# Asking for a block's rows at the head of the step, copying row numbers a block ahead, and placing filter pieces in the first half of the second product

## The chip, the cores and the metric

The kernel runs on one core of a Trainium2 chip. A core has a matrix engine (TensorE, PE in the profile; PEld are its weight loads), three engines for elementwise work (VectorE or DVE, ScalarE or ACT, GpSimd or POOL), and SyncE (SP), which here does nothing but issue transfers. Each engine works through its own queue in order; a wait at the head of a queue holds everything behind it. The metric is device time in microseconds, the median of several runs.

## The reference

Two stages follow each other: a mixing of each sequence by a filter in the frequency domain, and a layer of eight experts in which each token's expert is set by a hash of its id.

```python
X = np.fft.rfft(x, axis=1)                    # x: 8 batches, 2496 tokens, 256 channels
Y = X * (filt_r + 1j * filt_i)[None, :, :]
y = np.fft.irfft(Y, n=x.shape[1], axis=1)
tokens = y.reshape(19968, 256)
expert_idx = token_ids * np.int64(2654435761) % np.int64(8)
for e in range(8):
    mask = expert_idx == e
    h = np.maximum(tokens[mask] @ w1[e], 0.0)  # 256 -> 1024
    out[mask] = h @ w2[e]                      # 1024 -> 256
```

Everything is in 32-bit floats.

## The kernel before, in words

**The transform.** 2496 is 39 x 64, so each batch's transform is done as products with small matrices: a first product over 39 (stage1, `pa`), a second over 64 (forward, `pb`), the filter on VectorE (four operations a unit: L277, twice L281, L282), the second product back (back, `pc`), and the first one back (stage3, `pd`). From batch 2 on the order of the data is turned between products by a round trip through HBM: `d1` is written by GpSimd's queue and read back by load2 (L262, tile `mid`), `d2` is written at L301 and read back by load4 (L365, tile `t`). x itself comes by load1 (L208). Stage3 scatters the finished rows, with their token number behind them, into `xs` in HBM (L384, indirect DMAs of GpSimd), sorted by expert.

**The experts.** `xs` is cut into blocks of 256 rows of one expert (85 of them, 80 are certain to be used; the rest stands behind a branch on a count). A block becomes ready when all batches of its stage have been scattered: stages end with batch 2, 3, 4, 6 and 8 (`STAGES`), the stage of the last two batches begins with block 50. `step(i)` (L868) computes block i. Its parts:

- `load(i)` (L754): four transfers on SP (L760) bring the rows of block i into `xg`. There are two such buffers, so block i+2 goes into the buffer of block i.
- `numbers(i)` (L769): four small copies on GpSimd (L773) take the rows' token numbers out of `xg` into `no` (eight buffers), where the store later finds them.
- `token_parts(i)`, `token_sums(i)` (L776, L783): VectorE transposes the rows (L779, `xt`) and makes four sums of their quarters (L789, `st`).
- `weight_sums(i)` (L792): GpSimd makes four sums of quarters of w1 (L798, `tw`, two buffers each).
- `up(i)` (L801): the first product in seven quarter products (L808) instead of eight, put together by VectorE (L815) and ScalarE (L812, L819). It needs `xt`, `st`, w1 and `tw`.
- `down(i)` (L836): the second product (L841, 16 matmuls into one bank), copied out by VectorE (L846, `osb`).
- `store(i)` (L848): two indirect DMAs of GpSimd (L851) put the rows into the output.
- `weights(i, which)` (L397): SP loads w1 (L415) and w2 (L418) of block i, skipped where the expert is that of block i-2. There are two buffers of each, so w1 of block i+2 waits for up(i), and w2 for down(i).

**The order.** The order of instructions on every engine is the order in which Python calls them. Blocks 0 and 1 and all of batches 0 and 1 come before the first step. The work of batches 2 to 7 is cut into pieces with a due time in blocks (L732 to L737: `part1`, `part2`, `part3`). `within` (L667) moves each due time t into the second half of its step: t = 7.4 becomes 7.5 + 0.4 / 2 = 7.7. In step i the pieces due before i + .6 are issued ahead of the second product, those before i + .7, .8 and .9 after its first, second and third quarter, and those before i + 1 after the last.

In step i, SP's queue holds, in this order: the row load of block i+2, w1 of block i+2, loads of pieces, w2 of block i+2 and loads of late pieces. GpSimd's queue holds: weight sums of block i+1, the two stores of block i-1, the number copies of block i, then the pieces' writes and scatters. VectorE's: the work of up(i), transpose and token sums of block i+1, filters of the pieces, the copy of down(i).

Of the kernel before, what the change touches and what calls it, by code (L numbers as in the profile page):

```python
# [29 lines left out]
NS, NQ = N1 // 2 + 1, 64  # L30
# [4 lines left out]
SG = 4  # L35
# [8 lines left out]
NT = (N + E * (TB - 1)) // TB  # L44
# [75 lines left out]
def kernel(  # L120
# [276 lines left out]
    def weights(i, which):  # L397

        if i >= NT:
            return  # L400
        if i >= 2 and which == 0:
            ws[i] = ws[i - 2][0:2]
        eng, kw = nc.sync, {}
        if which == 0:
            ws[i].append(eng.value_load(chunk_i[0:1, 0, i:i + 1], min_val=0, max_val=E - 1))
            if i >= 2:
                ws[i].append(eng.value_load(chunk_i[0:1, 1, i:i + 1], min_val=0, max_val=1))
        e = ws[i][2]
        if i >= 2:
            kw = {"cond": ws[i][3]}  # L410
        if which == 0:


            for f in (slice(0, F // 2), slice(F // 2, F)) if i < 2 else (slice(0, F),):
                eng.dma_start(out=ws[i][0][:, :, f],  # L415
                              in_=moe_w1[bass.ds(e, 1)].rearrange("one (p dp) f -> p (one dp) f", p=P)[:, :, f], **kw)
        else:
            eng.dma_start(out=ws[i][1], in_=moe_w2[bass.ds(e, 1)].rearrange("one (fp p) d -> p (one fp) d", p=P), **kw)  # L418
# [19 lines left out]
    def load_tables(part):  # L438
        if part < 2:

            nc.gpsimd.tensor_copy(junk[:], first.x[2 * part][0:1, 0, 0:1])
        sl = S_PARTS[part]
        nc.sync.dma_start(out=d_t[:, sl, :], in_=d_dram.ap()[:, sl, :])
        for k in range(2):
            load_filter(k, sl)
# [218 lines left out]
    def spaced(t0, t1, n):  # L664
        return [t0 + (t1 - t0) * u / n for u in range(n)]

    def within(todo):  # L667

        return [(t // 1 + .5 + t % 1 / 2, piece) for t, piece in todo if t is not None]

    def part1(b, at, loads):
        bt = batches[b]
# [2 lines left out]

    def part2(b, at, loads, lag):
        bt = batches[b]
        return within([(at[u], lambda u=u: bt.forward(u)) for u in range(NS // 2)] +
                      [(at[u] + lag, lambda u=u: bt.back(u)) for u in range(NS // 2)] +
                      [(loads[g], lambda g=g: bt.load2(g)) for g in range(NS // SG)])  # L680

    def part3(b, at, loads):
        bt = batches[b]
# [8 lines left out]
    def chain(k):  # L692

        for step, j in ((Batch.turn2, k + 1), (Batch.back_c, k - 2), (Batch.forward, k)):
            if 0 <= j < NS:
                step(batches[j // (NS // 2)], j % (NS // 2))


    todo = [(t, lambda k=k: load_tables(k)) for k, t in enumerate((-160, -159, -157, -156))]
# [54 lines left out]
    def load(i):  # L754

        g = gath.tile([P, TB // 32, XW], F32, name=f"xg_{i}", tag="xg")
        rows = xs[tiles[i] * TB:(tiles[i] + 1) * TB, :]
        for q in range(4):
            w = C // 4 + (q == 3)
            ld = (nc.scalar if i < 2 and q % 2 else nc.sync).dma_start(  # L760
                out=g[32 * q:32 * q + 32, :, 0:w], in_=rows[:, 64 * q:64 * q + w].rearrange("(a t) c -> t a c", t=32))
            for b in range(STAGES[stage_of[i]], B):
                tc.declare_no_dep(ld.ins, group=f"xs_{b}", reason="the tiles of a stage hold tokens of its batches alone")
            if stage_of[i] < G - 1:
                tc.declare_no_dep(ld.ins, group="xs_pad", reason="places without a token lie in the last stage alone")
            tc.add_to_no_dep_group("xs_read", ld.ins)
        xg[i] = g

    def numbers(i):  # L769

        no = nums.tile([P, 2], I32, name=f"no_{i}", tag="no")
        for a in range(4):
            nc.gpsimd.tensor_copy(no[32 * a:32 * a + 32, :], xg[i][96:128, a::4, C // 4].bitcast(I32))  # L773
        to_rows[i] = no

    def token_parts(i, to=None):  # L776

        xt = work.tile([P, DP, 2, P], F32, name=f"xt_{i}", tag="xt")[:] if to is None else to
        nc.vector.transpose(out=xt.rearrange("p d h (a t) -> p (h a) d t", t=32),  # L779
                            in_=xg[i][:, :, 0:C // 4].rearrange("p a (c d) -> p a d c", d=DP))  # L780
        parts[i] = {(h, d): xt[:, d, h, :] for h in range(2) for d in range(DP)}

    def token_sums(i):  # L783
        x = parts[i]
        st = work.tile([P, 4, P], F32, name=f"st_{i}", tag="st")
        for k, (p, q, op) in enumerate((((1, 0), (1, 1), OP.add), (0, (0, 0), OP.subtract),
                                        ((0, 0), (1, 0), OP.subtract), ((0, 1), 1, OP.subtract))):
            p, q = [st[:, v, :] if isinstance(v, int) else x[v] for v in (p, q)]
            nc.vector.tensor_tensor(st[:, k, :], p, q, op=op)  # L789
        parts[i]["sums"] = st  # L790

    def weight_sums(i, eng=None):  # L792

        eng, w1, h = eng or nc.gpsimd, ws[i][0], F // 2
        b11, b12, b21, b22 = [w1[:, d, f * h:f * h + h] for d in range(DP) for f in range(2)]
        t = [tpool.tile([P, h], F32, name=f"tw_{i}_{k}", tag=f"tw{k}") for k in range(4)]
        for k, (p, q) in enumerate(((b12, b11), (b22, t[0][:]), (b22, b12), (b21, t[1][:]))):
            eng.tensor_tensor(t[k][:], p, q, op=OP.subtract)  # L798
        sums[i] = t

    def up(i, ht):  # L801
        w1, x, st, t = ws[i][0], parts[i], parts[i]["sums"], sums[i]
        ps = {k: banks[k].tile([P, 4, P], F32, name=f"up_{i}_{k}", tag=k) for k in "abc"}
        h11, h12, h21, h22 = [ht[:, h, 4 * f:4 * f + 4, :] for h in range(2) for f in range(2)]

        def product(bank, w, xx, first):
            for f in range(4):
                nc.tensor.matmul(out=ps[bank][:, f, :], lhsT=w[:, f * P:(f + 1) * P], rhs=xx,  # L808
                                 start=first and f == 0, stop=True, skip_group_check=True)

        def relu(out, in_):
            nc.scalar.activation(out=out, in_=in_, func=AF.Relu)  # L812

        def plus(out, bank, other):
            nc.vector.tensor_tensor(out, ps[bank][:], other, op=OP.add)  # L815

        h = F // 2
        product("a", w1[:, 0, 0:h], x[0, 0], True)
        nc.scalar.copy(out=h21, in_=ps["a"][:])  # L819
        product("c", t[0], st[:, 0, :], True)  # L820
        plus(h22, "c", h21)
        product("b", t[1], st[:, 1, :], True)
        plus(h12, "b", h21)
        product("a", w1[:, 1, 0:h], x[0, 1], False)
        relu(h11, ps["a"][:])
        product("b", t[2], st[:, 2, :], False)
        plus(h22, "b", h22)
        relu(h22, h22)
        product("c", w1[:, 1, h:], st[:, 3, :], False)
        plus(h12, "c", h12)  # L830
        relu(h12, h12)
        product("b", t[3], x[1, 1], False)
        plus(h21, "b", h21)
        relu(h21, h21)
# [13 lines left out]
    def store(i):  # L848
        o = rows.pop(i)
        for h in range(2):  # L850
            st = nc.gpsimd.indirect_dma_start(  # L851
                out=out[:], out_offset=bass.IndirectOffsetOnAxis(ap=to_rows[i][:, h:h + 1], axis=0),
                in_=o[:, h, :], in_offset=None, bounds_check=N - 1, oob_is_err=False)
            tc.declare_no_dep(st.ins, group="out_rows", reason="distinct rows")
            tc.add_to_no_dep_group("out_rows", st.ins)
# [3 lines left out]
    token_parts(0)  # L859
    token_sums(0)  # L860
    weight_sums(0, nc.vector)
    used = []

    def run_until(t):
        while main and main[0][0] < t:
            main.pop(0)[1]()

    def step(i):  # L868
        ht = work.tile([P, 2, FP, P], F32, name=f"ht_{i}", tag="ht")
        if i + 1 < NSURE:  # L870
            weight_sums(i + 1)
        if i > 0:
            store(i - 1)
        numbers(i)
        if i + 2 < NT:
            load(i + 2)
        up(i, ht)
        weights(i + 2, 0)
        if i + 1 < NSURE:
            token_parts(i + 1)  # L880
            token_sums(i + 1)
        run_until(i + .6)
        down(i, ht, lambda k: run_until(i + .7 + .1 * k) if k < 3 else None)
        weights(i + 2, 1)
        run_until(i + 1)
# [57 lines left out]
```

## Time and profile before

| | |
|---|---|
| median of 3 runs | 1681.69 us (1681.4 to 1684.31) |
| the profiled execution, whole | 1686.24 us |
| its span, first to last instruction | 1684.5 us |
| granted TensorE clock, mean | 0.943 |
| before the first step | 0 to 164.9 us |
| blocks 0 to 45, with the pieces of batches 2 to 7 | 164.9 to 1127.1 us |
| blocks 46 to 79, almost no pieces | 1127.1 to 1659.7 us |
| after the last certain block | 1659.7 to 1684.5 us |
| DMA engines' busy share, blocks 0 to 45 and 46 to 79 | 0.62, 0.29 |
| w1 and w2 (`wts`) transfers | 162 of 1024 KB, some of them skipped |

Where step i begins is read from the timeline: it is the start of the first of the 56 matmul records of L808 that belong to a block. A table of stretches gives, for each window of the span, how long each engine was busy in it and the clock that TensorE was granted. A line of waits reads "who, at which line, waited for whom: us in total, how often, the longest". "SPq" is SP's queue: its instructions issue transfers, and are not counted as busy.

### The profile page before, as it was taken

The numbers are of one execution on the slowest core, as the hardware profiler recorded it, in microseconds if no ns is written. First come the engines' busy times: TensorE is split into PE (matmuls) and PEld (weight loads), VectorE is DVE, ScalarE is ACT, GpSimd is POOL, SyncE is SP. The second block draws the span as 40 slices with busy tenths as digits, with TensorE's granted clock in tenths as the row PEclk, the third lists the DMA queues.
The fourth block names the chain that finished last, engine by engine and source line by source line (L and its number), as shares of the span: only waits on it lengthen the run. The fifth ranks groups of instructions, "written<-read, shape, count | busy, mean of one in ns | idle before, by whom it ended". The sixth has DMA issues, their size and how long they took to land. (4 is left out here: it accounts for less than half of the span.)

```text
span 1684.5 us, 24896 instructions
## 1 busy us (share of the span) xinstructions
PE 1477.6 (88%) x8746; PEld 1322.3 (78%) x8746; DVE 838.5 (50%) x1362; ACT 415.8 (25%) x710; POOL 888.8 (53%) x1120
## 2 busy tenths in 40 slices
PE   6976998879589989799899899999898998989894
PEld 6965887768488878678788789888787887888783
DVE  6842552545245556235555565343364554546263
ACT  3542232212123223222222222221121221212120
POOL 4156256655366457466454766665453555455353
PEclk9987999989799989899999999999899999999997
DMA  8245565745766496675654654443413222231412
GB/s 220 73 141 158 177 201 134 257 135 173 208 208 201 151 283 218 184 221 185 219 175 123 169 157 143 136 138 123 129 39 106 65 82 79 72 96 39 129 38 48
DMA packets 201673, 245.73 MB, mean 146 GB/s; under 512 B 105749, under 2 KB 170701, under 8 KB 194426
## 3 DMA queue, kind: packets, MB, share of 16 engines
q1 hardware_dynamic: 168919, 166.72, 35.3%
q0 software_dynamic: 28480, 73.44, 13.3%
q10 hardware_dynamic: 4147, 3.95, 0.8%
q8 instruction: 72, 1.18, 0.3%
q14 instruction: 55, 0.45, 0.1%
HBM read 251.19 MB, written 75.14 MB: 194 GB/s over the span
## 5 line engine op out<-in xcount | busy, mean ns | idle before, releaser
L841 PE MATMUL dps<-wts,ht 128*128 128x256 f32 x2560 | 584.6, 382 | 0.9 <-DMA wts<-in_moe_w_dram 0.9
L841 PEld LDWEIGHTS dps<-wts,ht 128*128 128x128 f32 x2560 | 485.5, 192 | 70.1 <-issue 4.7
L798 POOL TENSOR_TENSOR tw<-wts 128x512 f32<-128x512 f32 x158 | 203.3, 1287 | 358.5 <-DMA wts<-in_moe_w_dram 343.8
L815 DVE TENSOR_TENSOR ht<-up_b,ht 128x512 f32<-128x512 f32 x240 | 165.4, 689 | 166.4 <-PE up_b L808 140.7
L384 POOL DMA_INDIRECT xs<-o,sidx x176 | 177.2, 1007 | 94.0 <-issue 43.3
L808 PE MATMUL up_a<-xt,wts 128*128 128x128 f32 x1280 | 178.4, 284 | 48.4 <-DMA wts<-in_moe_w_dram 35.8
L808 PE MATMUL up_b<-st,tw 128*128 128x128 f32 x1280 | 183.7, 289 | 41.9 <-DVE ht L815 39.9
L808 PEld LDWEIGHTS up_a<-xt,wts 128*128 128x128 f32 x1280 | 168.2, 199 | 58.4 <-issue 48.7
L808 PEld LDWEIGHTS up_b<-st,tw 128*128 128x128 f32 x1280 | 164.1, 201 | 54.9 <-issue 35.5
L798 POOL TENSOR_TENSOR tw<-wts,tw 128x512 f32<-128x512 f32 x158 | 203.5, 1288 | 6.2
L812 ACT ACTIVATE ht<-ht 128x512 f32<-128x512 f32 x240 | 151.3, 631 | 195.4 <-DVE ht L815 177.9
L815 DVE TENSOR_TENSOR ht<-up_c,ht 128x512 f32<-128x512 f32 x160 | 110.1, 688 | 148.8 <-PE up_c L808 118.2
L851 POOL DMA_INDIRECT out_dram<-osb,no x160 | 161.2, 1007 | 41.6 <-issue 30.9
L773 POOL COPY no<-xg 32x2 int32<-32x2 int32 x340 | 63.3, 186 | 187.5 <-DMA out_dram<-osb,no 144.5
L819 ACT COPY ht<-up_a 128x512 f32<-128x512 f32 x80 | 46.9, 586 | 417.5 <-PE up_a L808 379.4
L779 DVE STREAM_TRANSPOSE xt<-xg 128x512 f32<-128x512 f32 x80 | 56.6, 708 | 173.1 <-DMA xg<-xs 173.1
L846 DVE COPY osb<-dps 128x512 f32<-128x512 f32 x80 | 54.9, 687 | 154.9 <-PE dps L841 115.9
L281 DVE TENSOR_TENSOR z<-pb,filt 64x512 f32<-64x512 f32 x160 | 110.2, 689 | 24.6 <-PE pc L294 14.0
L226 PE MATMUL pd<-t,wi_t 120*117 120x256 f32 x320 | 83.9, 409 | 40.6 <-DMA t<-d 38.1
L277 DVE TENSOR_TENSOR y<-pb,filt 128x512 f32<-128x512 f32 x80 | 55.1, 689 | 106.5 <-PE pb L271 91.0
L226 PEld LDWEIGHTS pd<-t,wi_t 120*117 120x117 f32 x320 | 61.0, 195 | 55.1 <-DMA t<-d 39.5
L812 ACT ACTIVATE ht<-up_a 128x512 f32<-128x512 f32 x80 | 47.8, 597 | 198.9 <-PE up_a L808 158.8
(145 smaller groups left out, 1637.0 us busy)
## 6 DMA issues: line engine op xcount, KB each, us to landing
wts<-in_moe_w_dram SPq DMA_DIRECT2D x162, 1024.0 KB
xg<-xs SPq DMA_DIRECT2D x253, 64.0 KB
mid<-d SPq DMA_DIRECT2D x60, 256.0 KB
d<-mid POOLq DMA_DIRECT2D x60, 256.0 KB
t<-d SPq DMA_DIRECT2D x12, 960.0 KB
x<-in_x_dram SPq DMA_DIRECT2D x36, 312.0 KB
d<-mid POOLq DMA_DIRECT2D x10, 960.0 KB
xg<-xs SPq DMA_DIRECT2D x83, 65.0 KB
```

The source lines that it names most:

```text
L226: nc.tensor.matmul(out=ps[0:cols * H, k, :], lhsT=w[:], rhs=src[:, 2 * i + k, :], start=True, stop=True)
L277: nc.vector.tensor_tensor(out=y[:], in0=ps[:], in1=f_t[0][:, sl, :], op=OP.mult)
L281: nc.vector.tensor_tensor(out=z[b], in0=ps[a], in1=f_t[1][64 * hi:64 * hi + 64, s1:s1 + 2, :], op=OP.mult)
L384: st = nc.gpsimd.indirect_dma_start(out=xs[:], out_offset=bass.IndirectOffsetOnAxis(ap=index, axis=0), in_=rows, in_offset=None, bounds_ch ...
L773: nc.gpsimd.tensor_copy(no[32 * a:32 * a + 32, :], xg[i][96:128, a::4, C // 4].bitcast(I32))
L779: nc.vector.transpose(out=xt.rearrange("p d h (a t) -> p (h a) d t", t=32), in_=xg[i][:, :, 0:C // 4].rearrange("p a (c d) -> p a d c", d=DP))
L798: eng.tensor_tensor(t[k][:], p, q, op=OP.subtract)
L808: nc.tensor.matmul(out=ps[bank][:, f, :], lhsT=w[:, f * P:(f + 1) * P], rhs=xx, start=first and f == 0, stop=True, skip_group_check=True)
L812: nc.scalar.activation(out=out, in_=in_, func=AF.Relu)
L815: nc.vector.tensor_tensor(out, ps[bank][:], other, op=OP.add)
L841: nc.tensor.matmul(out=ps[:, h, :], lhsT=ht[:, h, fp, :], rhs=w2[:, fp, :], start=(fp == 0), stop=(fp == FP - 1))
L851: st = nc.gpsimd.indirect_dma_start(out=out[:], out_offset=bass.IndirectOffsetOnAxis(ap=to_rows[i][:, h:h + 1], axis=0), in_=o[:, h, :], i ...
```

## The change

Three edits, all of them in the order of instructions.

In `step(i)` the row load of block i+2 moves from behind the number copy to the head of the step. The number copy is now that of block i+1, and stands in front of the weight sums and of the stores; the copy of block 0 is issued before the first step. For the last five blocks the loop behind the steps still copies the numbers itself (L894 before). `within` gets a share: the forward pieces of `part2` (second product and filter) are placed by t = 7.4 -> 7.5 + 0.4 x 0.3 = 7.62, that is between .5 and .8 of their step, so none of them stands behind the second product's first half. The other pieces keep 0.5.

```diff
-    def within(todo):
+    def within(todo, share=.5):
 
-        return [(t // 1 + .5 + t % 1 / 2, piece) for t, piece in todo if t is not None]
+        return [(t // 1 + .5 + t % 1 * share, piece) for t, piece in todo if t is not None]
...
     def part2(b, at, loads, lag):
         bt = batches[b]
-        return within([(at[u], lambda u=u: bt.forward(u)) for u in range(NS // 2)] +
-                      [(at[u] + lag, lambda u=u: bt.back(u)) for u in range(NS // 2)] +
-                      [(loads[g], lambda g=g: bt.load2(g)) for g in range(NS // SG)])
+        return (within([(at[u], lambda u=u: bt.forward(u)) for u in range(NS // 2)], .3) +
+                within([(at[u] + lag, lambda u=u: bt.back(u)) for u in range(NS // 2)] +
+                       [(loads[g], lambda g=g: bt.load2(g)) for g in range(NS // SG)]))
...
     weight_sums(0, nc.vector)
+    numbers(0)
     used = []
...
     def step(i):
         ht = work.tile([P, 2, FP, P], F32, name=f"ht_{i}", tag="ht")
+        if i + 2 < NT:
+            load(i + 2)
         if i + 1 < NSURE:
+            numbers(i + 1)
             weight_sums(i + 1)
         if i > 0:
             store(i - 1)
-        numbers(i)
-        if i + 2 < NT:
-            load(i + 2)
         up(i, ht)
```

## The prediction, made before the changed kernel had run

> **What bounds the kernel now.** I read the page's first part, then what each engine waited for, then the waits of SP's queue, then the timeline of a few blocks, and last the table of stretches. "Block i" is one tile of 256 rows, "step i" the code that computes it.
>
> TensorE is busy 88% of the span, so the page alone says "TensorE bound". The waits say that something else paces it. All engines' waits, then SP's queue:
>
> ```profile
> span 1684.5 us, 24896 instructions
> PE 1477.6 (88%) x8746; PEld 1322.3 (78%) x8746; DVE 838.5 (50%) x1362; ACT 415.8 (25%) x710; POOL 888.8 (53%) x1120
> POOL tw L798 <- DMA wts<-in_moe_w_dram: 343.8, 57, 20.9
> DVE xt L779 <- DMA xg<-xs: 173.1, 43, 17.9
> POOL no L773 <- DMA out_dram<-osb,no: 144.5, 69, 6.7
> PE up_b L808 <- DVE ht L815: 41.0, 30, 5.0
> PE pd L226 <- DMA t<-d: 38.1, 4, 15.5
> PE up_a L808 <- DMA wts<-in_moe_w_dram: 35.8, 12, 4.8
> ```
>
> ```profile
> SPq L760 <- POOL no L773: 910.3, 79, 17.1
> ```
>
> Read: us in total, times, longest. SP, which issues almost every load, stands more than half of the span at the row load (L760) until GpSimd has copied the row numbers (L773). GpSimd in turn stands 344 us until w1 has landed, a load that SP issues behind that row load. So there is a loop. Blocks 55 to 57 in the timeline (start, length, engine, line, operation, tiles, count, idle before and its end), SP first, then GpSimd:
>
> ```profile
> 1298.16 1.81 SPq L760 DMA_DIRECT2D xg<-xs  x4
> 1301.50 0.37 SPq L415 DMA_DIRECT2D wts<-in_moe_w_dram  x1
> 1316.69 1.81 SPq L760 DMA_DIRECT2D xg<-xs  x4
> 1320.03 0.09 SPq L415 DMA_DIRECT2D wts<-in_moe_w_dram  x1
> ```
>
> ```profile
> 1306.81 1.26 POOL L798 TENSOR_TENSOR tw<-wts 128x512 f32<-128x512 f32 x1 [8.67 <-DMA wts<-in_moe_w_dram]
> ...
> 1312.01 0.99 POOL L851 DMA_INDIRECT out_dram<-osb,no  x1 [0.15 <-issue]
> 1313.31 0.97 POOL L851 DMA_INDIRECT out_dram<-osb,no  x1 [0.30 <-issue]
> 1315.82 0.85 POOL L773 COPY no<-xg 32x2 int32<-32x2 int32 x4 [1.53 <-DMA out_dram<-osb,no]
> ```
>
> Row load at 1298.2, w1 at 1301.5, landed 1306.8 (5.3 us), weight sums 5.1 us, two stores 2.3 us, 1.5 us for their landing, copy 0.85 us, and only then the next row load at 1316.7: 18.5 us for one turn. Where the expert stays and w1 is skipped, a turn is about 5 us shorter. TensorE over two blocks, one without and one with such a load:
>
> ```profile
> 1243.90:1257.60 13.70, 13.61 (x90) 12.48 (x89) 8.09 (x11) 3.08 (x5) 6.85 (x10) 1.00 0.16 40
> 1287.30:1306.80 19.50, 14.34 (x89) 12.53 (x89) 5.75 (x11) 3.08 (x5) 7.67 (x10) 0.94 0.45 137
> 1306.78 2.05 PE L808 MATMUL up_a<-xt,wts 128*128 128x128 f32 x8 [4.75 <-DMA wts<-in_moe_w_dram]
> ```
>
> Columns of the table: length, then busy time of PE, PEld, DVE, ACT, POOL, then granted clock. A block that nothing holds up takes 13.7 us at full clock. A late w1 costs 4.75 us of idle, and then the product takes 2.05 us instead of 1.06.
>
> **What the Trainium skill says.** "DMA: Bandwidth & Descriptors", section on the anatomy of one SWDGE DMA: a semaphore wait happens on the issuing sequencer, and most of a DMA's fixed 2 us is the receipt of the landing. The trace agrees on both: SP's queue waits, not the DMA engines, and the 69 waits for a store's landing average 144.5 / 69 = 2.1 us. "TensorE: Matmul & The Clock Gate", Part 1: an idle window of about 3.4 us halves the clock. The trace agrees: after 4.75 us the first three products take 1306.78 to 1311.73 = 4.95 us instead of 3 x 0.97 = 2.9, so a restart costs 2 us. "GPSIMD Engine Reference", section 1: GpSimd shares SBUF interfaces with VectorE for two-input operations. The trace agrees: token sums (L789) take 0.29 us alone at 1302.5, but 1.31 to 1.35 us beside the weight sums at 1643.8.
>
> **The change part by part.** No work is added or dropped; it is order alone.
>
> *Row load first, number copy a block ahead.* In step i the load of block i+2 goes ahead on SP; its buffer needs number copy i, which now ran in step i-1, and the transpose of block i, done in step i-1 too. So SP no longer waits for GpSimd. Its queue becomes: row load (1.8 us of issue), w1 of i+2 after up(i), loads of the pieces, w2 of i+2 after down(i). In the last part w1 of i+2 goes out about 7 us into step i, where before it went out at 29 us (1301.5 for block 57, whose step 55 began at 1272.2), 22 us earlier. It lands by 12 us and is first needed by the weight sums in step i+1: the 5 us are hidden with a block to spare.
>
> On GpSimd the copy (0.85 us) stands before the weight sums. It waits for rows i+1, loaded a step before, and the built order still gives it a wait for indirect DMAs issued just before it: then the scatters of the last step, or stores a step old. I price that wait at 2.1 us as today's. Behind it stand the weight sums (5.1), the stores (2.6) and the pieces; TensorE waits for the sums. GpSimd's work without pieces is 0.85 + 2.1 + 5.1 + 2.6 = 10.7 us, under 13.7, so it is covered. Weight sums may run earlier, at up's end, right beside the token sums: 5.2 instead of 1.2 us on VectorE, from 8.2 to 13.4 us of the step, just inside 13.7. If that cover fails, the next up starts 1 to 2 us late.
>
> Blocks 46 to 79 have almost no pieces: from 1127.1 to 1659.7 us, 532.6 us for 34 blocks, 15.7 each. I take 13.9 (13.7 and 0.2 for leftover collisions): 34 x 13.9 = 472.6, a gain of 60.
>
> Blocks 0 to 45 (164.9 to 1127.1, 962 us): TensorE's idle there that comes from SP or GpSimd being late is 38.1 (third product's input, `t<-d`: its load stands behind the stuck row load on SP), 3.6 of the 7.6 us on `mid<-d`, 3.5 and 0.9 on weights, 6.6 and 2.1 on late filtered rows of VectorE: 54.8. Five of these gaps exceed 3.4 us: 5 x 2 = 10 for the clock. Together 65. Not all stays gained: with faster blocks the round trips of a batch through HBM have less time, and the DMA engines are already busy 62% of this stretch. I give a third back, 22. Gain 43; bounds 0 and 65. The long waits for `ht` in blocks 5, 7, 8 and 13 (4 to 5 us each) lie inside runs of scatters and stay.
>
> *Filter pieces early.* The 60 forward units (two products, four VectorE operations, about 2.8 us) move from anywhere in the down product to its first half: before it, after its first quarter, after its second. It frees VectorE before the next up: 0.6 to 1.1 us gaps on `ht` in seven blocks, 5.5 us. Against it, forward meets its load earlier: the 4.0 us wait in block 0 grows by a quarter of the product, 1.75 us. I put the sum at 2 us lost to 5 gained, and take 0.
>
> End (1659.7 to 1684.5): loads and copies behind the last blocks keep their order; 0.
>
> Sum: 1684.5 - 60 - 43 = 1581.5. The profiled execution took 1686.24, 1.74 over its span, so 1583.2; the median of the runs is 0.27% under the profiled one: 1579, say 1580.
>
> **The rivals.**
> *Last part only:* the batches' round trips, not SP, hold blocks 0 to 45, or DMA traffic moves the waits. For it: DMA share .79 and .86 in blocks 12 and 18. Against: the load of `t` in block 12 is issued at 447.6, 4 us after the stuck row load. 1684.5 - 60 = 1624.5, as a run 1622.
> *More than I take:* nothing is given back, and the short waits for VectorE go too: 1684.5 - 60 - 65 - 15 = 1545, as a run 1542.
> *Nothing:* the row load is held by another wait (scatters of its stage). Against: after every copy SP issues within 0.1 us, save at stage starts. 1682.
> *Slower:* the copy with its landing wait now stands in front of the weight sums, 2.1 + 0.85 = 2.95 us, in every block with scatters. If GpSimd is then more than a block behind, each of the 46 early blocks pays it: 136 us, less 60 and with none of the 43: 1684.5 + 76 = 1760. It decides from the point where copy, sums, stores and pieces exceed the block's length, about 18 us there; in sum it is slower than before only if more than 60 / 2.95 = 20 of the early blocks pay and the 43 fails too. Against: GpSimd is busy 546 of 962 us, 11.9 a block, and in blocks 15 to 17 the sums end 4 to 14 us before the block does.
>
> **How the numbers follow.** Forecast 0.55, last part only 0.25, more 0.11, nothing 0.03, slower 0.06. Range 1540 to 1632: from all of the middle gained to none of it and 10 us lost on top. 0.2%, 3.4 us, is about what a measurement of this kernel can tell: faster 0.91, same 0.03, slower 0.06.
>
> **What would show it.** SP's wait for the copy falls from 910 to under 100 us; GpSimd's for w1 from 344 to below 100; TensorE's for w1 to about 3; blocks 46 to 79 take 13.7 to 14.1 us each. Wrong if the late blocks stay above 15 us, if waits for `t<-d` stay at 38 us, or if TensorE starts to wait for `tw`.

## The result, and the profile after

The changed kernel takes 1562.41 us, median of 4 runs (1554.48 to 1566.28); the kernel before took 1683.0 us beside it. The ratio is 0.9277, 95% interval 0.9237 to 0.9317. The profiled execution spans 1564.6 us, where before it was 1684.5: 119.9 us less.

The first part of the page, and what the engines waited for (us in total, times, longest):

```profile
span 1564.6 us, 24884 instructions
...
PE 1438.1 (92%) x8746; PEld 1293.3 (83%) x8746; DVE 804.3 (51%) x1362; ACT 415.4 (27%) x710; POOL 897.2 (57%) x1120
```

```profile
POOL no L773 <- DMA xs<-o,sidx: 104.2, 24, 11.9
POOL no L773 <- DMA out_dram<-osb,no: 80.1, 34, 7.8
...
PE up_b L808 <- DVE ht L815: 36.7, 17, 15.8
POOL tw L798 <- DMA wts<-in_moe_w_dram: 33.2, 12, 6.1
...
PE up_c L808 <- POOL tw L798: 12.1, 3, 10.0
...
DVE xt L779 <- DMA xg<-xs: 3.2, 1, 3.2
```

And what SP's queue waited for:

```profile
SPq L418 <- PE dps L841: 482.5, 61, 15.6
SPq L415 <- PE up_c L808: 102.5, 55, 5.2
...
SPq L760 <- POOL no L773: 8.7, 5, 4.2
```

SP stood 910.3 us at the row load for GpSimd's copy; now it is 8.7. It still waits, but for TensorE, until a weight buffer has been read: that is what a queue that runs ahead of the work looks like. The waits that hung on its loads shrank with it: GpSimd's for w1 from 343.8 to 33.2, VectorE's for rows from 173.1 to 3.2. TensorE's waits for `t<-d` (38.1) and for w1 (35.8) are no longer in the list. One is new: 12.1 us for the weight sums, 10.0 of them at one place.

The loop of the last part, around the same blocks. First SP and GpSimd in the timeline of the kernel after (start, length, engine, line, operation, tiles, count, idle before and its end):

```profile
1295.81 2.21 SPq L760 DMA_DIRECT2D xg<-xs  x4
...
1296.23 1.27 POOL L798 TENSOR_TENSOR tw<-wts,tw 128x512 f32<-128x512 f32 x1
...
1297.65 1.00 POOL L851 DMA_INDIRECT out_dram<-osb,no  x1 [0.15 <-issue]
...
1302.99 1.02 POOL L773 COPY no<-xg 32x2 int32<-32x2 int32 x4 [3.06 <-DMA out_dram<-osb,no]
...
1309.09 1.81 SPq L760 DMA_DIRECT2D xg<-xs  x4
```

Two row loads lie 13.3 us apart instead of 18.5, and the second goes out 5 us after the number copy has ended, no longer 0.02 us behind it: it starts when TensorE has ended a block.

The two stretches of the run, blocks 0 to 45 and 46 to 79, in the table of stretches, before and then after (columns: length, busy time of PE, PEld, DVE, ACT, POOL, granted clock, DMA share, GB/s):

```profile
164.92:1127.10 962.18, 868.03 (x5009) 773.21 (x5010) 477.45 (x790) 243.71 (x420) 545.95 (x667) 0.95 0.62 183
1127.10:1659.70 532.60, 484.59 (x2997) 439.84 (x2995) 265.75 (x371) 105.16 (x172) 265.92 (x347) 0.96 0.29 83
```

```profile
164.48:1073.80 909.32, 851.22 (x5009) 760.92 (x5010) 468.02 (x790) 243.34 (x420) 559.49 (x681) 0.97 0.67 196
1073.80:1540.00 466.20, 463.60 (x2997) 424.63 (x2995) 241.38 (x370) 105.07 (x172) 263.40 (x337) 1.00 0.33 92
```

Length less PE's busy time is TensorE's idle time. In the late blocks it went from 48.0 to 2.6 us, and the same 2997 products became 21.0 us shorter, with the granted clock at 1.00 instead of 0.96: together 66.4. In the early blocks idle went from 94.2 to 58.1 and the products became 16.8 us shorter: 52.9. That is 119.3 of the 119.9 us. Nearly every late block now takes 13.6 us, and TensorE idles 2.6 us in all 34 of them together; of the idle time in blocks, what is left lies almost all in blocks 0 to 45.

Three stalls make up 33.2 of the 58.1 us left there: block 8 with 15.8 us of idle time, block 25 with 10.0 and block 6 with 7.3. In block 25, TensorE, SP and GpSimd in the timeline:

```profile
698.43 0.99 POOL L384 DMA_INDIRECT xs<-o,sidx  x1 [0.30 <-issue]
...
706.05 0.85 POOL L773 COPY no<-xg 32x2 int32<-32x2 int32 x4 [6.63 <-DMA xs<-o,sidx]
706.93 1.82 SPq L760 DMA_DIRECT2D xg<-xs  x4
706.99 1.26 POOL L798 TENSOR_TENSOR tw<-wts 128x512 f32<-128x512 f32 x1
...
708.30 1.44 PE L808 MATMUL up_c<-st,tw 128*128 128x128 f32 x5 [10.04 <-POOL tw L798]
```

GpSimd, behind with its scatters, comes to the number copy; the copy waits 6.63 us for scatters to land; behind it stand the weight sums that TensorE needs now. In block 8, VectorE and TensorE:

```profile
356.20 0.69 DVE L277 TENSOR_TENSOR y<-pb,filt 128x512 f32<-128x512 f32 x1 [14.03 <-DMA xs<-blank,at_i]
...
359.10 0.69 DVE L846 COPY osb<-dps 128x512 f32<-128x512 f32 x1
359.71 0.68 DVE L815 TENSOR_TENSOR ht<-up_c,ht 128x512 f32<-128x512 f32 x1
...
361.13 1.19 PE L808 MATMUL up_b<-st,tw 128*128 128x128 f32 x4 [15.81 <-DVE ht L815]
```

The blank tile, whose content is scattered to the padding places, comes from the pool of three buffers that the filtered rows `y` and `z` use. VectorE's next filtered row needs that buffer and waits 14.03 us until the fourteen scatters have landed; the sums for TensorE stand behind it in VectorE's queue. The kernel before had this wait too, 8.5 us long. In block 6, which takes 27.9 us where it took 18.6 before, VectorE and TensorE again:

```profile
304.45 0.69 DVE L815 TENSOR_TENSOR ht<-up_b,ht 128x512 f32<-128x512 f32 x1 [6.50 <-remote]
...
305.28 2.04 PE L808 MATMUL up_b<-xt,tw 128*128 128x128 f32 x8 [5.16 <-DVE ht L815]
```

GpSimd issues scatters one behind the other from 293 to 303 us, and VectorE stands still for 6.50 us among them. The profile names no instruction of this program that ended that wait ("remote"). This standstill comes up again in the experiments.

### The profile page after: what moved, and what is told of

The parts are those of the page before. It is cut to its first block, busy times and chain, and to the rows that moved or that the text cites. A ratio compares the mean times of both kernels' runs of the same rounds, so it can differ in the third digit from the quotient of the medians.

```text
span 1564.6 us, 24884 instructions
## 1 busy us (share of the span) xinstructions
PE 1438.1 (92%) x8746; PEld 1293.3 (83%) x8746; DVE 804.3 (51%) x1362; ACT 415.4 (27%) x710; POOL 897.2 (57%) x1120
## 4 chain that ended last, share of the span: by engine, by line
PE 79%; DMA 7%; issue 5%; DVE 4%; POOL 2%; another core or an unknown queue 1%; ACTq 0%; ACT 0%; POOLq 0%; SPq 0%; DVEq 0%
PE dps L841 32%; PE up_b L808 14%; PE up_c L808 8%; PE up_a L808 8%; PE pb L271 4%; PE pd L226 4%; PE pc L294 3%; PE pa L226 3%; DMA xs<-o,sidx 2%; DMA out_dram<-osb,no 1%; DMA d<-mid 1%; DMA wts<-in_x_dram 1%; DVE z L281 1%; DVE ht L815 1%
## 5 line engine op out<-in xcount | busy, mean ns | idle before, releaser
L798 POOL TENSOR_TENSOR tw<-wts 128x512 f32<-128x512 f32 x158 | 203.6, 1289 | 39.2 <-DMA wts<-in_moe_w_dram 33.2
L808 PE MATMUL up_b<-st,tw 128*128 128x128 f32 x1280 | 178.2, 283 | 32.7 <-DVE ht L815 29.6
L773 POOL COPY no<-xg 32x2 int32<-32x2 int32 x340 | 65.8, 194 | 242.7 <-DMA xs<-o,sidx 104.2
L808 PEld LDWEIGHTS up_b<-st,tw 128*128 128x128 f32 x1280 | 158.2, 194 | 44.7 <-issue 18.2
L808 PE MATMUL up_a<-xt,wts 128*128 128x128 f32 x1280 | 170.8, 277 | 4.4 <-issue 4.4
L808 PEld LDWEIGHTS up_a<-xt,wts 128*128 128x128 f32 x1280 | 163.6, 194 | 9.7 <-issue 5.6
L281 DVE TENSOR_TENSOR z<-pb,filt 64x512 f32<-64x512 f32 x160 | 110.2, 689 | 24.9 <-PE pc L294 21.5
L808 PE MATMUL up_b<-xt,tw 128*128 128x128 f32 x640 | 91.6, 287 | 7.3 <-DVE ht L815 7.1
L808 PE MATMUL up_c<-st,tw 128*128 128x128 f32 x640 | 86.6, 279 | 12.1 <-POOL tw L798 12.1
L808 PEld LDWEIGHTS up_b<-xt,tw 128*128 128x128 f32 x640 | 78.9, 194 | 18.4 <-issue 8.1
```

The source lines that it names most:

```text
L281: nc.vector.tensor_tensor(out=z[b], in0=ps[a], in1=f_t[1][64 * hi:64 * hi + 64, s1:s1 + 2, :], op=OP.mult)
```

## The experiments

Each kernel was run in turn with the kernel before on one chip. Chips differ (the kernel before took 1683 and 1679 us in the first two groups, 1655 and 1682 in the last two), so kernels of different groups are compared by ratio, and single blocks by the profiles. There is one profile of each kernel, and the runs of one kernel differ by up to 19 us, so a few us in a single block prove nothing by themselves. Blocks are counted from the start of one block's first product to the next one's.

| kernel | group | ratio to before | 95% interval | span, us | blocks 0 to 45 | blocks 46 to 79 |
|---|---|---|---|---|---|---|
| before | | 1 | | 1684.5 | 962.2 | 532.6 |
| after | | 0.9277 | 0.9237 to 0.9317 | 1564.6 | 909.3 | 466.2 |
| e1_order_alone | 1 | 0.9213 | 0.9173 to 0.9253 | 1555.5 | 899.5 | 466.0 |
| e2_filter_alone | 1 | 1.0043 | 1.0025 to 1.0061 | 1690.0 | 966.5 | 533.5 |
| e4_copy_behind | 1 | 0.9221 | 0.9178 to 0.9264 | 1553.3 | 900.5 | 463.6 |
| e5_pads_33 | 1 | 0.922 | 0.9179 to 0.9261 | 1559.5 | 900.1 | 469.5 |
| e10_copy_head | 2 | 0.9171 | 0.9137 to 0.9205 | 1529.8 | 885.0 | 465.1 |
| e8_w1_behind_w2 | 2 | 0.96 | 0.9561 to 0.964 | 1609.6 | 955.1 | 469.6 |
| e7_copy_dve | 2 | 0.908 | 0.9051 to 0.9109 | 1518.8 | 881.6 | 463.6 |
| e6_pads_spread | 2 | 0.9272 | 0.9242 to 0.9302 | 1562.4 | 908.9 | 469.1 |
| e9_dve_no_share | 3 | 0.9053 | 0.9022 to 0.9085 | 1496.7 | 870.0 | 463.6 |
| e11_pads_40 | 3 | 0.9083 | 0.9052 to 0.9115 | 1502.3 | 873.5 | 463.7 |
| e12_pads_last | 4 | 0.9051 | 0.9027 to 0.9074 | 1518.7 | 875.5 | 464.0 |

### One half at a time: e1_order_alone and e2_filter_alone

e1 is the changed kernel with `.3` left out, so that the filter pieces stand where they stood; e2 is the kernel before with `.3` alone.

```diff
-        return (within([(at[u], lambda u=u: bt.forward(u)) for u in range(NS // 2)], .3) +
+        return (within([(at[u], lambda u=u: bt.forward(u)) for u in range(NS // 2)]) +
```

> The new order without the filter edit (forward pieces again over the whole second half of their step). Theory: the gain is SP's queue freed from GpSimd, and the filter pieces bring almost nothing; then about 1562 us (1553 to 1572), SP's wait for the number copy under 30 us, blocks 46 to 79 at 13.6 us. Rival: the filter edit carries half of the middle's gain; then 1585 us or more.

> The filter edit alone on the kernel before. Theory: about 1681 us (1672 to 1690), SP's wait for the number copy stays above 850 us, blocks 46 to 79 stay at 15.7 us. Rival: 1655 us or less.

Measured: the order alone 1552.99 us, at the lower edge of what was expected, and the filter places alone 1692.21, 2 us above it. The order carries the whole gain, and the early filter pieces cost rather than nothing: 0.43% (0.25 to 0.61) on the kernel before, some 7 us. On the new order the difference, 0.9277 to 0.9213, is of the same sign and size, but those two intervals overlap, and by the profiles it is block 25 alone (29.4 us against 17.6). What TensorE waited for with the filter places alone (the kernel before had 41.0, 38.1, 35.8 and 7.6 in these rows):

```profile
PE up_b L808 <- DVE ht L815: 58.5, 37, 14.4
PE pd L226 <- DMA t<-d: 29.5, 3, 16.7
PE up_a L808 <- DMA wts<-in_moe_w_dram: 28.9, 11, 4.8
PE pb L271 <- DMA mid<-d: 23.3, 3, 11.2
```

Two rows grew by 33.2 us and two fell by 15.5; in blocks 0 to 45 TensorE's idle time grew from 94.2 to 104.0 us. The row of `mid<-d` fits pieces that meet their data earlier, before it has landed. That the waits for `ht` grew because four VectorE operations now stand in front of what TensorE needs is a reading, not shown: the longest of them, 14.4 us, is in block 8, where the padding is.

### Where the copy must stand: e10_copy_head and e4_copy_behind

e10 is the kernel before, and only the copy of the block's own numbers moves to the head of the block, not a block ahead. e4 is the changed kernel, its copy a block ahead but behind the weight sums and stores.

```diff
     def step(i):
         ht = work.tile([P, 2, FP, P], F32, name=f"ht_{i}", tag="ht")
+        numbers(i)
         if i + 1 < NSURE:
             weight_sums(i + 1)
         if i > 0:
             store(i - 1)
-        numbers(i)
```

> The kernel before with one thing moved: the number copy of block i goes from behind the weight sums and the stores to the head of block i's own step on GpSimd (not a block earlier), load and filter pieces as before. Theory (SP's queue is held by where the copy stands in GpSimd's queue, and any place ahead of the weight sums frees it): GpSimd reaches the head of step i while TensorE is still in block i-1, so the row load still goes out at the end of block i-1 or soon after; SP's wait for the copy falls from 910 to under 200 us, blocks 46 to 79 at 13.6 to 14.0 us, median 1550 to 1572 as with the order alone (1553). Rival (the copy must be a whole block ahead): SP still waits some 400 us or more, blocks 46 to 79 above 14.5, median 1600 or more.

```diff
         if i + 1 < NSURE:
-            numbers(i + 1)
             weight_sums(i + 1)
         if i > 0:
             store(i - 1)
+        if i + 1 < NSURE:
+            numbers(i + 1)
```

> The changed kernel with the number copy of block i+1 behind the weight sums and the stores instead of ahead of them; the row load stays at the head. Theory: the copy waits for the landing of the last scatters, and in front of the weight sums this costs TensorE the 10.0 us in block 25 and about 1 us each in blocks 22 and 27 (waits of up_c for tw) and a restart of the clock; then about 1549 us (1542 to 1556) and TensorE waits for tw under 3 us. Rival: the sums are late for another reason (w1, or GpSimd's work itself), or the wait moves onto the scatters behind it; then 1558 us or more.

e10 took 1538.05 us, faster than I expected, and ahead of the changed kernel (the intervals lie apart). It has the filter pieces in their old places, so its like is e1, and those two intervals overlap. No whole block of lead is needed. SP's queue there:

```profile
SPq L760 <- POOL no L773: 222.5, 36, 14.8
```

SP still stands 222.5 us, a little over my bound, 194 of it in blocks 0 to 45. These take 885.0 us all the same, no longer than e1's 899.5, where SP's wait for the copy is 6.7 us in all; the late blocks take 465.1. A quarter of the old wait remained and the whole gain came, so the sum of an engine's waits is no measure of cost. What counted is how often the loop had to turn. In the kernel before, the row load of block i+2 waits, through the copy and the weight sums ahead of it, for w1 of block i+1, which SP issues right behind the row load of block i+1: one turn for each block, 18.5 us where a block needs 13.7. In e10 and e4 the sums ahead of the copy are those of block i, so a turn has two blocks of time, and in the changed kernel three. This is read from the order of the code; the runs agree with it.

e4 took 1555.10 us, inside the range of its theory. It has no wait of TensorE for GpSimd's weight sums, and block 25 takes 17.2 us instead of 29.4, as expected; but block 25 takes 17.1 to 17.6 in e1, e5 and e6 as well, with the copy ahead of the sums. Only the changed kernel and e8 below (30.1) show the stall. So a copy ahead of the sums is not enough for it; GpSimd must be late there as well, and whether it is changed with every shift of the pieces around it. e4's interval overlaps the changed kernel's, so the time does not settle what the place of the copy costs. A copy in either place frees SP.

The diff also moves the row load to the head of the step. That is no move in any queue: between its old place and its new one stand only GpSimd's instructions, and SP's own order (row load, w1, w2) is the same. This follows from the code; it was not run by itself, but e10 has the row load in its old place and the whole gain.

### Which load carries the gain: e8_w1_behind_w2

The changed kernel, but w1 of block i+2 is issued behind w2 of block i+2. In the changed kernel w2 is issued 7.9 us after w1 in the late blocks and 10.5 in the early ones (medians), so w1 is late by about that.

```diff
-        weights(i + 2, 0)
+        weights(i + 2, 0, False)
...
         weights(i + 2, 1)
+        weights(i + 2, 2)
```

(The second argument 2 issues w1; `False` keeps only the reading of the expert's number in the old place.)

> The changed kernel with one load made late on purpose: w1 of block i+2 is issued after w2 of block i+2, so at the end of block i instead of 7 us into it. Theory (w1 has a block to spare since SP is free; the gain is that it goes out early enough, not as early as possible): issued 14 us into block i it has about 14.6 us until TensorE needs the sums, of which two loads of 1 MB side by side take 5 to 10 and the sums 5.2: on time or up to 2 us late where the expert changes, nothing where it stays; median 1562 to 1600, blocks 46 to 79 at 13.7 to 14.7. Rival (w1's moment paces the loop, so 7 us later gives most of the gain back): 1620 to 1680, blocks 46 to 79 above 15.

Measured 1613.86 us, above the theory's range and just under the rival's. The blocks say that each is right in one half. Blocks 46 to 79 take 469.6 us, 3.4 more than after: there w1 has the spare time that the theory gave it. Blocks 0 to 45 take 955.1, 45.8 more, nearly the 962.2 of before. What TensorE waited for there (lines are one later in this kernel):

```profile
PE pd L226 <- DMA t<-d: 13.7, 2, 8.0
PE up_c L809 <- POOL tw L799: 13.1, 5, 11.3
PE up_a L809 <- DMA wts<-in_moe_w_dram: 12.1, 3, 9.6
```

In blocks with filter pieces this delay gives back 87% of what they had gained. It is not all w1: 13.7 of the 38.9 us in these rows are waits for `t`, which SP loads too, and 11.3 are the stall in block 25 that the changed kernel has as well. Which part of the 45.8 us is w1 coming late, and which the changed order of SP's loads, was not separated.

### The copy off GpSimd: e7_copy_dve

```diff
-            nc.gpsimd.tensor_copy(no[32 * a:32 * a + 32, :], xg[i][96:128, a::4, C // 4].bitcast(I32))
+            nc.vector.tensor_copy(no[32 * a:32 * a + 32, :], xg[i][96:128, a::4, C // 4].bitcast(I32))
...
         if i + 1 < NSURE:
-            numbers(i + 1)
             weight_sums(i + 1)
...
             token_parts(i + 1)
+            numbers(i + 1)
             token_sums(i + 1)
```

> The changed kernel with the number copies of block i+1 on VectorE, beside the transpose of block i+1, instead of on GpSimd: no copy and no wait for a landing stands ahead of the weight sums. Theory (a copy that waits for scatters to land delays the weight sums by up to 7 us and caused the 10 us stall for tw in block 25): that stall is gone, TensorE waits for tw under 3 us in all, median 1545 to 1557. Rival (the four copies on VectorE push the token sums of a loaded VectorE back by as much): the stall goes, but waits for st or ht grow, median 1558 to 1570, blocks 46 to 79 above 13.8.

Measured 1525.08 us, better than either expected, and 2% under the changed kernel with intervals well apart. e1 and e9 below, which differ in the same edit but have the filter pieces in their old places, say the same: 0.9213 and 0.9053. VectorE carries the 340 copies (0.36 us each) in its spare time: the late blocks take 463.6 us. No copy waits for a landing ahead of GpSimd's weight sums any more (2.0 us of such a wait are left in the sums themselves), and blocks 0 to 45 take 27.7 us less than after. Of these 10.9 are block 25, and another 9.4 are block 6, which takes 18.5 us instead of 27.9: VectorE does not stand still there. Block 6 took 27 to 29 us in e1, e5, e6, e8 and e10 too, all with the copy on GpSimd ahead of the weight sums, and 24.9 in e4 with the copy behind them; why, no run shows. TensorE's waits for VectorE's and GpSimd's sums:

```profile
PE up_b L808 <- DVE ht L815: 17.2, 14, 3.9
...
PE up_a L808 <- POOL tw L798: 4.1, 1, 4.1
...
PE up_b L808 <- POOL tw L798: 1.4, 1, 1.4
```

The 4.1 us are the very first block's.

### The padding: e5_pads_33, e6_pads_spread, e11_pads_40, e12_pads_last

Block 8 is the longest block of the changed kernel. Four kernels move its fourteen padding scatters; e5 and e6 start from the changed kernel, e11 and e12 from e9 below.

In e5 they are due at 33, in e11 at 40.4:

```diff
-    todo += [(-137.2, places), (-128, tile_experts), (-121, experts), (-80, blanks), (7.4, pads)]
+    todo += [(-137.2, places), (-128, tile_experts), (-121, experts), (-80, blanks), (33, pads)]
```

In e6 there is one piece for each scatter, with a blank tile of its own; in e12 the 27.1 is 41.05, and all share one blank tile:

```diff
+    todo += [(27.1 + q / 2, lambda q=q: pads(q)) for q in range(NQP)]
...
-    def pads():
-        blank = ppool.tile([P, 2 * C], I32, name="blank", tag="p")[:, 0:W]
+    def pads(q):
+        blank = ppool.tile([P, 2 * C], I32, name=f"blank_{q}", tag="p")[:, 0:W]
...
-        for q in range(NQP):
-            scatter(blank.bitcast(F32), at_i[:, q:q + 1], "xs_pad")
+        scatter(blank.bitcast(F32), at_i[:, q:q + 1], "xs_pad")
```

> The changed kernel with the 14 scatters of padding rows due at 33 instead of 7.4, where no filter piece is near. Theory: their source tile takes one of the three buffers of the filtered rows, VectorE waits at the next filter until all 14 have landed, and this is the 15.8 us of TensorE's idle in block 8; then that wait is gone, about 1545 us (1538 to 1552). Rival: a long run of scatters stalls VectorE and ScalarE wherever it stands; then blocks 33 to 35 show the stall and the time is 1558 us or more.

> The changed kernel with the 14 padding scatters spread over blocks 27 to 33, two in a block, each with a blank tile of its own that is given back when it has landed, instead of 14 in a row in block 7. Theory (two things stall TensorE in a padding run: VectorE waits for the blank tile's buffer, 14 us in block 8, and VectorE and ScalarE also stand still while a long run of scatters goes out, 10 us in block 34 of the kernel with all of it there): both are gone, block 8 near 22 us, blocks 27 to 34 within 1 us of the changed kernel's, median 1540 to 1553. Rival (each scatter costs VectorE and ScalarE about 1 us wherever it stands): the 14 to 20 us come back spread over blocks 27 to 34, median 1555 to 1565.

e5 took 1554.74 us, between the ranges of theory and rival, and e6 1557.14, inside the rival's. In both, block 8 falls from 39.6 to 22.2 us, and something nearly as long appears where the scatters went. In e6 the mistake is mine: each scatter's blank tile still comes from the pool of the filtered rows, and those are still made there. The list of who waited for the blank tile (us, times):

```profile
  DVE blank L641: 12.5, 1
  DVE z L281: 10.2, 4
```

Block 28 takes 29.2 us instead of 15.3, and the ratio is the changed kernel's. In e5 it is another thing. Block 34 takes 28.0 us instead of 15.3. In its timeline:

```profile
851.55 0.59 ACT L819 COPY ht<-up_a 128x512 f32<-128x512 f32 x1 [7.16 <-PE dps L841]
...
852.19 1.06 PE L808 MATMUL up_b<-st,tw 128*128 128x128 f32 x8
...
855.57 0.69 DVE L815 TENSOR_TENSOR ht<-up_c,ht 128x512 f32<-128x512 f32 x1 [4.27 <-PE up_a L808]
...
863.27 0.69 DVE L815 TENSOR_TENSOR ht<-up_b,ht 128x512 f32<-128x512 f32 x1 [7.01 <-issue]
864.08 1.78 PEld L808 LDWEIGHTS up_b<-st,tw 128*128 128x128 f32 x8 [10.13 <-issue]
```

Scatters went out from 845.5 to 863.1 us. VectorE's sum at 863.27 needs the product that ran from 852.19 to 853.25; it starts 7 us after the operation before it, and the profile knows of nothing that it waited for. Nobody in this profile waits for the blank tile's buffer. What holds it is open.

> The same with the 14 padding scatters in block 40, behind the last filter pieces and ahead of the first load of the last stage (step 48). Theory (in block 8, and in the spread version in block 28, VectorE waits for a buffer of the filtered rows that the blank tile holds until its scatters have landed; with no filter piece behind it nobody needs the buffer): block 8 falls from 36 to about 22 us and blocks 40 to 42 gain at most 3 us, median 1497 to 1509. Rival (what stands still is VectorE and ScalarE themselves during a run of scatters, as in block 34 of the version with the scatters there, where no buffer was waited for): blocks 40 and 41 grow by 8 to 14 us, median 1509 to 1520.

1504.41 us, but the kernel before is faster on this chip too (1654.85), so the time decides nothing, and the blocks are as neither side said. Block 8 falls from 35.4 to 23.0 us, as expected. Here no filtered row follows, and VectorE and ScalarE work on through the run of scatters (926 to 944 us): block 40, in which it begins, takes 14.5 us in both. That speaks against the rival's standstill wherever a run of scatters is. But block 41 takes 31.6 us instead of 15.3, more than block 8 gave. GpSimd, then SP and TensorE, in its timeline:

```profile
926.31 0.97 POOL L384 DMA_INDIRECT xs<-blank,at_i  x1 [5.96 <-DVE blank L642]
...
942.88 0.97 POOL L384 DMA_INDIRECT xs<-blank,at_i  x1 [0.30 <-issue]
943.86 1.14 POOL L301 DMA_DIRECT2D d<-mid  x2
...
947.21 0.36 SPq L365 DMA_DIRECT2D t<-d  x1
...
954.61 2.91 PE L226 MATMUL pd<-t,wi_t 120*117 120x256 f32 x6 [14.07 <-DMA t<-d]
```

ScalarE had the piece `mid` ready at 924.5 us, but its transfer to HBM is issued by GpSimd, behind fourteen scatters of 1.28 us: 19 us later. "DMA: Bandwidth & Descriptors" of the Trainium skill, section on the anatomy of one SWDGE DMA, says that a transfer waits on the sequencer that issues it, not in the DMA engines. Here that sequencer had nothing to wait for; it was fourteen instructions behind, and the transfer was as late as its queue.

> As the version with copies on VectorE and the old filter places, but the 14 padding scatters go out two in a block in blocks 41 to 47, behind the last filter piece (no buffer of filtered rows is needed any more, no write of a batch's second product waits behind them on GpSimd) and ahead of the first load of the last stage. Theory (the padding has no price of its own: what it cost, 14 to 17 us in blocks 8, 28, 34 and 41, is what stood behind it each time): block 8 falls from 35 to about 23 us, blocks 41 to 47 grow by less than 3 us in all, profiled span 10 to 14 us under that of the same version with the padding in block 7, ratio 0.896 to 0.901. Rival (14 scatters cost some 12 us wherever they stand, through the DMA engines or through VectorE and ScalarE): blocks 41 to 47 grow by 8 us or more, ratio 0.903 to 0.909.

1520.71 us. With the same scatters two in a block, behind all of that, blocks 41 to 47 grow by 3.9 us in all, not by 12, and block 8 takes 23.0. That is just over the theory's 3 and far from the rival's 8, so by these blocks the padding itself costs little; what stood behind it paid. But the whole did not follow: the ratio is 0.9051 where e9 has 0.9053, so the expected 0.896 to 0.901 is missed. Other blocks of the profile (7, 13 and 26) were 3.5, 1.5 and 4.4 us longer than in e9's, on another chip. Whether e12 is faster than e9 is not settled.

### The best version: e9_dve_no_share

e7 with the filter pieces in their old places (the diff of e1).

> The changed kernel with both corrections together: number copies on VectorE beside the transpose, and the filter pieces where the kernel before had them (.5 in place of .3). Theory (the early filter pieces cost 7 to 10 us of their own, as seen with them alone and with the order alone, whoever copies the numbers): ratio to before 0.908 - 0.006 = 0.902, median 1511 to 1520 against 1525 with the early pieces. Rival (the cost of early pieces came from the copy on GpSimd waiting for scatters, the stall in block 25, and is gone with it): 1521 to 1530.

1498.81 us on a chip where the kernel before takes 1654.85: the microseconds can't be set beside the forecast, and by ratio, 0.9053 to e7's 0.908, the intervals overlap and the ranges of theory and rival both reach into e9's. The profiles give blocks 0 to 45 11.6 us less than in e7. With e1 and e2 that is the third pair in which the early filter pieces lose, by 4 to 12 us; only the pair of e2 is clear of noise. It is the fastest version, level with e12: 2.2 points under the changed kernel.

## Why the prediction was right, and where not

The forecast was 1580 us, range 1540 to 1632, and 1562.41 came. Of its span, 1581.5, 16.9 us are missing: 6.4 in the late blocks, 9.9 in the early ones, 0.6 elsewhere.

*SP's queue and the loop: right, and shown.* SP's wait fell from 910 to 8.7 us, late blocks went to 13.7 us each (466.2 / 34), a gain of 66.4 where 60 was forecast. The term that was off is the "0.2 for leftover collisions": it is nothing; nearly every late block takes 13.6 us. e10 adds that the loop, and not the length of SP's wait, was the cost.

*Early blocks: gain right within 10 us (52.9 for 43), made up otherwise.* The idle time of 54.8 was to go and did not wholly: TensorE's idle fell by 36.1. The clock was under-priced: five restarts at 2 us made 10, the products became 16.8 us shorter. And the give-back of 22 us was put in the wrong place. I took it for "round trips of a batch through HBM"; but waits for `t<-d` went from 38.1 to none. What came back as idle time were block 25 (10.0 us, none before), block 6 (7.3, 0.4 before) and block 8 (15.8, 10.6 before): 22.1 in all, the size of the forecast by luck. Block 25 has the very mechanism of the rival "slower": a copy with its landing wait in front of the sums, GpSimd behind. It held in one block where the rival needed more than twenty. TensorE's waits for `tw`, up to 12.1 us, are also what I had named as a sign of being wrong: the cover of 10.7 us under 13.7 was worked out without the pieces, and with them it failed there.

*The landing wait at 2.1 us: mis-sized.* Its new place is among scatters: the waits for them average 104.2 / 24 = 4.3 us, the longest 11.9. "DMA: Bandwidth & Descriptors" of the Trainium skill, in the same section, gives about 2 us as the constant part of a DMA, most of it the receipt. The copy's waits for stores are near that (2.1 us before, 80.1 / 34 = 2.4 after), those among scatters are not; the profile does not split a wait into its parts. e7, which takes the copy and its wait off GpSimd, measures what they cost there: 0.9277 to 0.908, some 33 us. In the two profiles the blocks differ by 30.3 us, and only the 10.9 of block 25 are a wait of TensorE for GpSimd's sums.

*Filter pieces at 0: wrong.* They cost 7 us on the kernel before (e2). Both terms of the sum failed: the "5 gained", for TensorE's waits for VectorE's `ht` did not shrink but grew from 41.0 to 58.5, and the "2 lost", for those for `mid<-d` grew by 15.7, where I had 1.75 for one of them. Part of this was offset by shorter waits for `t<-d` and w1.

*"Hidden with a block to spare": right in the late blocks, where it was said of.* With w1 some 8 us later they lose 3.4 us (e8). The early blocks, with theirs some 10 us later, lose 45.8.

*"The long waits for `ht` stay": right in sum, 41.0 to 36.7, by luck.* TensorE's idle time in blocks 5, 7 and 13 fell from 4.2 to 4.8 us each to at most 1.1; block 8's grew, and block 6 came new. I took all for runs of scatters. Block 8's is a buffer: the blank tile holds one that VectorE needs.

## What to carry to other kernels

When one queue issues most loads, look for what its head waits for, and whether that in turn waits for a load behind it; here each of three places for the copy that gave the loop more than one block for a turn brought the gain, and the wait's length said little. An instruction that reads a loaded buffer and then frees it did better here on an engine that issues no transfers. A block of transfers that "can go anywhere" cost here what stood behind it: in a buffer's pool, in an engine's queue, or in the data that a later stage reads.

## What the runs showed of the hardware that was not expected

- VectorE and ScalarE at times stand still during a run of GpSimd's scatters, with no instruction that the profile shows as their wait: VectorE for 7.01 us at 863.27 in e5, for 6.50 at 304.45 after, and for 5 to 7 us in block 6 of e5, e6, e8 and e10; ScalarE for 13.33 us at 865.47 in e5. Its cause is open. A run of scatters is not enough: in e11 fourteen of them left both engines alone. Nor are busy DMA engines: their share was 0.25 to 0.30 during that run and 0.92 to 1.00 from 845 to 856 us in e5, but it was 1.00 over block 6 of the kernel before as well (298 to 304 us), without a standstill.
- The copy's waits for scatters to land took 4.3 us on average and up to 11.9, twice what its waits for stores took in the kernel before. The profiles give no time from issue to landing for either.
- The kernel before took 1655 us on one chip and 1679 to 1683 on others, so whole times can't be compared across chips. Most of the difference lies ahead of the first step, whose code hardly differs: it starts at 147.5 and 149.6 us in the profiles of the first chip (e9, e11) and at 163.8 to 165.7 in those of groups 1 and 4. A ratio to the kernel before carries this too, so it is not exact from chip to chip either.
